# The last stage of a fused attention and MoE kernel: instructions of three engines kept in program order, with another layout of the work in a unit

## The chip, the cores and the metric

One core of one Trainium2 chip runs the whole kernel. The metric is device time in microseconds (us). Before the change the median of three runs is 1489.99 us (1488.47 to 1503.18).

## What is computed

Everything is float32. Attention through 32 packed tokens per head gives 4608 rows of 512 numbers. Two dense blocks follow; the change is in the second.

```python
out = sm_attn(q, sm_attn(p, k, v), sm_attn(p, k, v))   # 8 batches, 8 heads, 576 rows, 64 wide
x = transpose_and_reshape(out)                          # 4608 x 512
r = maximum(x @ w_in, 0);  x = (s * r * r + b) @ w_out  # 512 -> 2048 -> 512
a = x @ w1;  b = x @ w2                                 # 512 -> 1024 each
out = (a * b @ w3) @ w_out2                             # 1024 -> 1024 -> 512
```

## The kernel before

Each float32 operand is split into two parts of fewer bits, hi and lo (`split`, L77 to L81: a cast on ScalarE, ACT, writes hi; a subtraction on VectorE, DVE, writes lo), and each product is three matmuls on TensorE, PE (`mm3`, L83 to L88: lo by hi, hi by lo, hi by hi). Large products use seven smaller ones instead of eight (a Strassen-like scheme), so sums and differences of blocks are formed on DVE beforehand and afterwards.

The kernel has three stages. The first two (attention and the first dense block) take the time up to about 853 us and are left alone. The last stage has three parts.

**w3 times w_out2.** Both weights are multiplied once, so that every row of data meets one matrix in place of two. The loop `for n, m in enumerate(VM)` takes eight blocks of 128 rows of w3. For each, `load_w3` fetches a block two steps ahead, `V_tr` transposes it on PE into PSUM (tile w4t) and splits it into w3T, and `V_mm` runs 24 matmuls of 512 columns into the PSUM tile w4a; from that the seven combinations of the product are formed and split (w4c). At the first step the loop also loads the first piece of the data (`load_x`, tile xb) and eight tiles of weights (`load_w`, tile whl, 256 KB each).

**Units.** The rows are taken in NB3 = 6 pieces j of 768, and each piece in 8 units i of 128 columns of a and b. A unit is seven products (`prod`, 6 x 7 = 42 matmuls of 384 columns, in the order 0, 1, 5, 4, 6, 3, 2) into four PSUM tiles X, Z, Y_ and W. Product 5 adds onto X after ACT has copied X (Ta, L1152), product 6 adds onto it after ACT has copied it again (Ta, L1159), and product 2 adds onto Y_ after DVE has added Y_ to the copy Tb (L1149 behind L1164). At the unit's end DVE multiplies Ta by Tb (L1178) into the tile CA (units 0 to 3) or CB (units 4 to 7). In the last unit of a piece the seven operands of the next piece are split (`split_x`, tile xc).

**y.** The seven products of the previous piece's a * b with w4c are put between the products of a unit as fillers: a chunk (`y_chunk`) is 12 matmuls of 256 columns for one 128-row tile t, three chunks make one of the seven products n, and `y_fin` moves the result out of PSUM (tile yps) into the output sums O. `y_prep` splits the operand of a product into two tiles op of a ring of four; `y_sums` forms the sums of CA and CB (L1187 to L1192). After the last unit of the last piece nothing is left to fill, and the 21 chunks run by themselves: this is the tail. There each chunk is moved out of PSUM by itself.

What sets the order: each engine runs its instructions in the order of the built program, and a scheduler that plans with estimated durations chooses that order. An instruction handed to `tc.keep_in_program_order` stays in the order of the source against the others so marked on its engine. Before the change this holds in the last stage for the first matmul of each product from the second unit on and for the y matmuls, and for nothing on ACT and DVE. All loads and stores here go through one queue of SyncE, SP, in order.

Of the kernel before, what the change touches and what calls it, by code (L numbers as in the profile page):

```python
# [16 lines left out]
ALU = mybir.AluOpType  # L17
# [5 lines left out]
def fused_kernel(  # L23
# [142 lines left out]
    if True:  # L166
# [267 lines left out]
        def pp_split(bp):  # L434
# [3 lines left out]
            for o in range(2):  # L438
                for bb in range(2):
                    c = slice(64 * (bb ^ o), 64 * ((bb ^ o) + 1))  # L440
                    split(hi[:, o::2, c], lo[:, o::2, c], ppT[:, bp, o::2, bb, :], pin=True)
# [502 lines left out]
        def V_tr(m, ps_of):  # L944
            for half in range(2):
                w3T[m, half] = wch_p.tile([P, 2, 4, P], F32R, tag="wph", name="w3T", bufs=4)
                ps = ps_of("w4t")
                for c in range(4):
# [5 lines left out]
                      w3T[m, half][:, 1].rearrange("p a b -> p (a b)"), ps)  # L954
# [103 lines left out]

        def comb_x(j, part):
# [4 lines left out]
            if part == 0:  # L1064
                t1, t2 = (
                    (dec if j == 0 else p3["w4"]).tile(
                        [P, 2, TH], F32, tag="raw" if j == 0 else "xt", name="xt",
                        bufs=RAWB if j == 0 else 2,
                    )
                    for _ in range(2)  # L1070
                )
# [6 lines left out]
        def split_x(j, pr):  # L1078
            src = xt[j][pr]
            if pr == 3:  # L1080
                tt(out=src, in0=src, in1=xt[j][5], op=ALU.subtract)
            t = bp_.tile([P, 2, 2, TH], F32R, tag="xc", name="xc", bufs=7)
            split(t[:, 0], t[:, 1], src)
            xc[j, pr] = t

        def V_mm(m):
            ps = p_ps("w4a")
            for c in range(FB2):
                w = w3T[m, c // 4]
                mm3(ps, w[:, 0, c % 4, :], w[:, 1, c % 4, :],  # L1090
                    *wo2[c], c == 0, c == FB2 - 1)
            i = m % KH
            if m < KH:
# [3 lines left out]
                nc.scalar.copy(p3["b12"], ps[:, NH:])  # L1097
                tt(out=p3["T"][:, 0], in0=p3["b12"], in1=ps[:, :NH], op=ALU.subtract)
                split(w4c[i][:, 0, 0], w4c[i][:, 1, 0], ps[:, :NH])
            else:  # L1100
# [5 lines left out]
                      w4c[i][:, 1, 1:3].rearrange("p a c -> p (a c)"), ps)  # L1106
                split(w4c[i][:, 0, 3:7], w4c[i][:, 1, 3:7], T)
# [21 lines left out]
        O = w4.tile([P, 4, TT, NH], F32, name="O")  # L1129
        C, Y, ops = {}, {}, {}  # L1130

        def prod(j, i, pr, ps, first):
            w = whl.pop((j * FB2 + i, pr))
            for k in range(2):
# [3 lines left out]
                    first and k == 0, k == 1, i + j > 0, skip_group_check=not first)  # L1138
            load_w()

        def unit(j, i, fill, after):
# [10 lines left out]
            nc.scalar.copy(Ta[:, 0], X[:, :TH])  # L1152
            after(0)
# [172 lines left out]
```

## Time and profile before

| | us |
|---|---|
| median of three runs | 1489.99 |
| the profiled execution: its own time | 1485.32 |
| its span | 1483.5 |
| PE busy | 1429.8 |
| DVE busy | 933.9 |
| ACT busy | 756.6 |

The span is one profiled execution, and 1.8 us lie around it. Busy times say which engine works most, not what a wait costs. Matmuls overlap, so how fast PE goes is read from the distance between the starts of matmuls. A wait that PE has is read from the table of waits; the chain of waits shows in order of time what released what.

### The profile page before, as it was taken

The page shows a single profiled execution, that of the slowest core. Times are in us where ns is not written, and L with a number is a line of the kernel's source. Part 1 is how long each engine was busy: PE and PEld are TensorE (multiplying, and loading weights), DVE is VectorE, ACT ScalarE, POOL GpSimd, SP SyncE. Part 2 cuts the span into 40 slices and gives each one's busy share as a digit, 9 for nine tenths or more (in the row PEclk, how much of TensorE's full clock was granted, in tenths as well). Part 3 has the DMA queues.
Part 4 walks back from the last instruction along what each step waited for, and adds up shares of the span by engine and source line. Part 5 has one row for each costly group of instructions (what it writes and reads, how often), then busy time and mean ns, then how long its engine had stood idle before and what let it go on. Part 6 is the DMA issues. An engine that isn't in the chain of part 4 may idle for free.

```text
span 1483.5 us, 28116 instructions
## 1 busy us (share of the span) xinstructions
PE 1429.8 (96%) x10858; PEld 1340.2 (90%) x10858; DVE 933.9 (63%) x1847; ACT 756.6 (51%) x1629; POOL 3.8 (0%) x38
## 2 busy tenths in 40 slices
PE   8999999999999999999999989989999999999996
PEld 5668999999999899998999978989989999899996
DVE  5879544665656766668878364475664856647553
ACT  3677555776566766568766442233422434224322
POOL 0000000000000000000000000000000000000000
PEclk8999999999999999999999999999999999999999
DMA  9967420242353542355635162765756757666541
GB/s 255 253 224 205 128 66 25 63 111 83 98 163 108 162 123 84 111 185 164 201 112 201 59 228 82 241 205 157 227 178 178 233 158 227 177 181 185 160 128 43
DMA packets 179365, 228.87 MB, mean 154 GB/s; under 512 B 55328, under 2 KB 115744, under 8 KB 179232
## 3 DMA queue, kind: packets, MB, share of 16 engines
q1 hardware_dynamic: 179232, 227.07, 51.8%
q8 instruction: 86, 1.41, 0.4%
q14 instruction: 47, 0.39, 0.1%
HBM read 182.98 MB, written 44.04 MB: 153 GB/s over the span
## 4 chain that ended last, share of the span: by engine, by line
PE 88%; DVE 4%; DMA 3%; ACT 2%; issue 1%; SPq 1%; POOL 0%; DVEq 0%; POOLq 0%; ACTq 0%
PE xps L84 9%; PE xps L88 9%; PE xps L87 9%; PE prod L84 7%; PE prod L88 7%; PE prod L87 7%; PE hps L84 4%; PE hps L88 4%; PE hps L87 4%; PE yps L84 4%; PE yps L87 4%; PE yps L88 4%; PE s1p L348 2%; PE scp L202 2%; PE ktp L330 1%; PE ktp L332 1%
## 5 line engine op out<-in xcount | busy, mean ns | idle before, releaser
L88 PE MATMUL xps<-gh,wo 128*128 128x288 f32 (+1 forms) x1024 | 302.5, 299 | 0.0
L87 PE MATMUL xps<-gl,wo 128*128 128x288 f32 (+1 forms) x1024 | 302.3, 298 | 0.0
L84 PE MATMUL xps<-gh,wo 128*128 128x288 f32 (+1 forms) x1024 | 292.0, 300 | 1.6 <-DVE wo L81 1.6
L84 PE MATMUL prod<-xc,whl 128*128 128x384 f32 x672 | 227.7, 339 | 19.3 <-DVE Tb L1149 16.8
L88 PE MATMUL prod<-xc,whl 128*128 128x384 f32 x672 | 225.8, 336 | 0.0
L87 PE MATMUL prod<-xc,whl 128*128 128x384 f32 x672 | 225.6, 336 | 0.0
L87 PEld LDWEIGHTS xps<-gl,wo 128*128 128x128 f32 x1024 | 193.3, 189 | 3.0 <-issue 1.4
L88 PEld LDWEIGHTS xps<-gh,wo 128*128 128x128 f32 x1024 | 193.0, 189 | 2.8 <-issue 1.9
L84 PEld LDWEIGHTS xps<-gh,wo 128*128 128x128 f32 x1024 | 188.5, 189 | 5.0 <-POOL gh L693 2.0
L689 ACT ACTIVATE r<-hps 128x288 f32<-128x288 f32 x256 | 104.4, 410 | 135.2 <-PE hps L88 131.7
L701 DVE TENSOR_TENSOR gl<-r,gh 128x288 fp32r<-128x288 f32 x256 | 115.3, 454 | 78.1 <-ACT r L698 75.5
L84 PE MATMUL hps<-ATh,wpl 128*128 128x288 f32 x512 | 153.9, 301 | 5.9 <-ACT r L689 5.1
L88 PE MATMUL hps<-ATh,wph 128*128 128x288 f32 x512 | 153.0, 299 | 0.0
L87 PE MATMUL hps<-ATl,wph 128*128 128x288 f32 x512 | 152.8, 298 | 0.0
L84 PE MATMUL yps<-w4c,op 128*128 128x256 f32 x504 | 142.3, 282 | 9.8 <-DVE O L1232 2.7
L84 PEld LDWEIGHTS prod<-xc,whl 128*128 128x128 f32 x672 | 126.7, 189 | 25.4 <-DVE Tb L1149 21.7
L1149 DVE TENSOR_TENSOR Tb<-Tb,prod 128x384 f32<-128x384 f32 x96 | 53.0, 553 | 149.6 <-ACT Tb L1164 145.6
L87 PE MATMUL yps<-w4c,op 128*128 128x256 f32 x504 | 142.2, 282 | 0.0
L88 PE MATMUL yps<-w4c,op 128*128 128x256 f32 x504 | 142.2, 282 | 0.0
L87 PEld LDWEIGHTS prod<-xc,whl 128*128 128x128 f32 x672 | 126.8, 189 | 0.0
L88 PEld LDWEIGHTS prod<-xc,whl 128*128 128x128 f32 x672 | 126.7, 189 | 0.0
L698 ACT ACTIVATE r<-r 128x288 f32<-128x288 f32 x256 | 112.6, 444 | 4.8
(166 smaller groups left out, 2582.9 us busy)
## 6 DMA issues: line engine op xcount, KB each, us to landing
whl<-whl SPq DMA_DIRECT2D x336, 256.0 KB, 3.0
raw<-in_moe_w_dram SPq DMA_DIRECT2D x32, 512.0 KB, 4.6
raw<-in_moe_w_out_dram SPq DMA_DIRECT2D x24, 512.0 KB, 4.4
x<-win SPq DMA_DIRECT2D x48, 256.0 KB, 2.8
v<-in_v_dram SPq DMA_DIRECT2D x16, 576.0 KB, 7.0
q<-in_q_dram SPq DMA_DIRECT2D x72, 128.0 KB, 4.4
x<-xst SPq DMA_DIRECT2D x16, 576.0 KB, 3.2
out_dram<-O SPq DMA_DIRECT2D x72, 128.0 KB, 2.4
```

The lines of the kernel that those rows point to most:

```text
L84: ins = nc.tensor.matmul(ps, wl, xh, start=start, stop=False, **kw)
L87: nc.tensor.matmul(ps, wh, xl, start=False, stop=False, **kw)
L88: nc.tensor.matmul(ps, wh, xh, start=False, stop=stop, **kw)
L202: nc.tensor.matmul(ps[sl, c:c + 64], qT[b, t][:, pr, sl], ppT[:, b // 2, pr, b % 2, :], start=True, stop=True,)
L330: nc.tensor.matmul(ps, zero[:, :P], zero, start=True, stop=True)
L332: nc.tensor.transpose(ps[:, jj * TP:(jj + 1) * TP], src[:, 2 * jj:2 * jj + 2, :].rearrange("p j d -> p (j d)"), ident[:TP, :TP],)
L348: nc.tensor.matmul(ps[par][NP * h:NP * (h + 1), :HS], pTd[u // 4][rows, u % 4, NP * h:NP * (h + 1)], kT[u][rows, h], start=True, stop=True,)
L689: nc.scalar.activation(r, ps[:, :HS], AF.Relu)
L698: nc.scalar.activation(r, r, AF.Square)
L701: nc.vector.tensor_tensor(out=gl[:, :HS], in0=r, in1=gh[:, :HS].bitcast(F32), op=ALU.subtract)
L1149: tt(out=out, in0=a, in1=ps[:, :TH], op=ALU.add)
```

## The change

Five things change, all in the last stage.

1. In the last stage every copy, split, sum and add on ACT and DVE, and every first matmul of a product, is kept in the order of the source (helpers `tt` and `cp`, and `pin=True` for `split`).
2. The side work of a unit is given by tables: `FILL` says which chunk of y runs at which of three places of which unit, `SIDE` which operands are split, which sums are formed and where the next piece's differences (`comb_x`) stand. The y work of a piece is spread from the end of unit 0 to unit 6 of the next piece. Before, it stood in units 1 to 6, and at a unit's edges.
3. Of each unit the operands of y are split right behind the copy of product 0, in both halves; the sums stand behind product 5 or product 4.
4. In the tail, products 4 and 5 get PSUM tiles of their own, product 7 starts a fresh one, and the results are moved out once per product or half of it, behind the operands of a later product.
5. The first weight tiles are loaded three at a time in steps 1 to 3 of the w3 loop, and there are nine buffers for them in place of eight.

```diff
-        nc.vector.tensor_tensor(out=lo, in0=src, in1=hi.bitcast(F32), op=ALU.subtract)
+        ins = nc.vector.tensor_tensor(out=lo, in0=src, in1=hi.bitcast(F32), op=ALU.subtract)
+        if pin and pin != "hi":
+            tc.keep_in_program_order(ins)
...
-        WPB = 8
+        WPB = 9
...
-        tt = nc.vector.tensor_tensor
+        def tt(out, in0, in1, op):
+            tc.keep_in_program_order(nc.vector.tensor_tensor(out=out, in0=in0, in1=in1, op=op))
+
+        def cp(out, src):
+            tc.keep_in_program_order(nc.scalar.copy(out, src))
...
         for n, m in enumerate(VM):
...
-                for _ in range(WPB):
+            if n + 1 < FB2:
+                V_tr(VM[n + 1], p_ps, True)
+            if n in (2, 3):
+                comb_x(0, n - 2)
+            if 4 <= n < 4 + 4:
+                for pr in PO[2 * n - 8:2 * n - 6]:
+                    split_x(0, pr)
+            V_mm(m)
+            if 1 <= n < 4:
+                for _ in range(3):
                     load_w()
-            if n + 1 < FB2:
-                V_tr(VM[n + 1], p_ps)
-            V_mm(m)
-            if n in (1, 2):
-                comb_x(0, n - 1)
-            if 3 <= n < 3 + 4:
-                for pr in PO[2 * n - 6:2 * n - 4]:
-                    split_x(0, pr)
...
         def y_tile(n, tail):
-            if n == 4 and tail:
-                a, b = p_ps("yps"), p_ps("yps")
-                return (a, a, b), a
+            if tail and n in (4, 5):
+                return tuple(p_ps("yps") for _ in range(2))
...
+        FILL = {(0, 2): (2, 0)}
+        for e, c in enumerate((n, t) for n in YO[1:] for t in range(TT)):
+            if e:
+                u, f = divmod(e + 2, 3) if e < 15 + 1 else divmod(e + 3, 3)
+                FILL[u, f] = c
+        for t in range(TT):
+            FILL[FB2 - 1, t] = (1, t)
+        SIDE = {
+            (0, 0): (("prep", 2),), (0, 5): (("sum", 1),),
+            (1, 0): (("prep", 4),), (1, 2): (("sum", 3),), (1, 3): (("sum", 2),),
+            (2, 0): (("prep", 6),), (2, 2): (("sum", 4),),
+            (3, 0): (("prep", 7),),
+            (4, 0): (("prep", 5),), (4, 3): (("comb", 0),),
+            (5, 0): (("prep", 3),), (5, 3): (("comb", 1),),
+            (6, 0): (("prep", 1),),
+        }
...
+                        xs = {0: (0,), 1: (1,), 2: (5, "t4"), 3: (4,), 4: (6,), 5: (3,), 6: (2,)}
...
-        for t in range(TT):
-            y_chunk(j, 1, t, True)
-        y_fin(j, 1)
-        for n in YO[1:]:
-            y_prep(j, n)
-            y_sums(j, n)
+        def chunks(n):
             for t in range(TT):
                 y_chunk(j, n, t, True)
-                y_fin(j, n, t)
...
+        chunks(1)
+        y_prep(j, 2)
+        y_sum(j, 1)
+        y_prep(j, 4)
+        fins(1, (), 0)
+        chunks(2)
...
+        chunks(6)
+        fins(6, (2, 3))
+        y_prep(j, 3)
+        fins(6, (), 1)
+        chunks(7)
+        fins(7, (2, 3), hf=1)
+        chunks(3)
+        fins(3, (1,), hf=0)
```

Up to the last stage the built program has the same instructions in the same order on every engine. In the last stage it has the same matmuls. Three places show what moved.

The first place is SP's queue at the start of the w3 loop, from the last load of the first piece's data on (xb is the data, w3st a block of w3, whl the weights of the units). Before:

```order
L1054 DMA xb<-x_1_0_75 128x192
L1041 DMA whl<-whl_89 128x512 x7
L1041 DMA whl<-whl_90 128x512
L942 DMA w3st<-w_5_102 128x1024
L942 DMA w3st<-w_2_99 128x1024
L1054 DMA xb<-x_1_0_75 128x96
L1054 DMA xb<-x_1_1_76 128x288
```

After:

```order
L1062 DMA xb<-x_1_0_75 128x192
L944 DMA w3st<-w_5_102 128x1024
L1049 DMA whl<-whl_89 128x512 x3
L944 DMA w3st<-w_2_99 128x1024
L1049 DMA whl<-whl_89 128x512 x4
L1049 DMA whl<-whl_90 128x512 x2
L944 DMA w3st<-w_6_103 128x1024
L944 DMA w3st<-w_3_100 128x1024
L1062 DMA xb<-x_1_0_75 128x96
L944 DMA w3st<-w_7_104 128x1024
```

The block w_5 now stands ahead of the weight tiles, and these are spread between the blocks of w3.

The second place is DVE at the border of two pieces: from the last product of the unit 7 of a piece (CB is written from Ta and Tb) to the end of unit 0 of the next. Before:

```order
L1178 TENSOR_TENSOR CB<-Ta,Tb 128x2x384
L81 TENSOR_TENSOR xc<-xb,xc 128x768
L1187 TENSOR_TENSOR S_12274<-CA,CB 128x1536
L1149 TENSOR_TENSOR Ta<-Ta,prod 128x384
L81 TENSOR_TENSOR op<-CB,op 128x768 x2
L1072 TENSOR_TENSOR xt<-xb 128x768
L81 TENSOR_TENSOR op<-CB,op 128x768
L1189 TENSOR_TENSOR CA<-CA 128x1536
L1149 TENSOR_TENSOR Tb<-Tb,prod 128x384
L1073 TENSOR_TENSOR xb<-xb 128x2x384
```

After:

```order
L1029 TENSOR_TENSOR CB<-Ta,Tb 128x2x384
L81 TENSOR_TENSOR xc<-xb,xc 128x768
L81 TENSOR_TENSOR op<-CB,op 128x768 x2
L1029 TENSOR_TENSOR Ta<-Ta,prod 128x384
L1029 TENSOR_TENSOR Tb<-Tb,prod 128x384 x2
L1029 TENSOR_TENSOR S_12276<-CA,CB 128x1536
L1029 TENSOR_TENSOR Ta<-Ta,prod 128x384
L1029 TENSOR_TENSOR CA<-Ta,Tb 128x2x384
```

Between CB and the first add into Tb there were a split of xc, the sum S, an add into Ta, three splits of op, one difference xt and the sum CA; there are now a split of xc, two splits of op and one add into Ta. On ACT three casts of op stood in a row between the two copies into Ta there, and two do now.

The third place is DVE in the tail, from the last CB on. Before:

```order
L1178 TENSOR_TENSOR CB<-Ta,Tb 128x2x384
L1187 TENSOR_TENSOR S_12274<-CA,CB 128x1536
L81 TENSOR_TENSOR op<-CB,op 128x768
L1189 TENSOR_TENSOR CA<-CA 128x1536
L81 TENSOR_TENSOR op<-CB,op 128x768
L1232 TENSOR_TENSOR O<-O,yps 128x256
L81 TENSOR_TENSOR op<-CB,op 128x768
L1190 TENSOR_TENSOR CA<-S_12274,CA 128x1536
L1232 TENSOR_TENSOR O<-O,yps 128x256
L81 TENSOR_TENSOR op<-CA,op 128x768
L1232 TENSOR_TENSOR O<-O,yps 128x256
L81 TENSOR_TENSOR op<-CA,op 128x768
```

After:

```order
L1029 TENSOR_TENSOR CB<-Ta,Tb 128x2x384
L81 TENSOR_TENSOR op<-CB,op 128x768 x2
L1029 TENSOR_TENSOR S_12276<-CA,CB 128x1536
L81 TENSOR_TENSOR op<-CB,op 128x768 x2
L1029 TENSOR_TENSOR CA<-CA 128x1536
L81 TENSOR_TENSOR op<-S_12276,op 128x768 x2
L1029 TENSOR_TENSOR CA<-S_12276,CA 128x1536
L1029 TENSOR_TENSOR O<-O,yps 128x768
L81 TENSOR_TENSOR op<-CA,op 128x768 x2
L1029 TENSOR_TENSOR CA<-CB,CA 128x1536
```

The moves out of PSUM (O) stood between the operands of the same product, one per 128-row tile; they now stand behind the operands of a later product, mostly whole.

## Rows read from the trace of the kernel before

**Rows 1.** The page: its head and busy time by engine.

```profile
span 1483.5 us, 28116 instructions
...
PE 1429.8 (96%) x10858; PEld 1340.2 (90%) x10858; DVE 933.9 (63%) x1847; ACT 756.6 (51%) x1629; POOL 3.8 (0%) x38
```

**Rows 2.** Busy time by stretch: stretch, length, engines, granted clock, DMA share, GB/s.

```profile
870.90:875.40 4.50, 4.41 (x15) 3.86 (x16) 4.50 (x7) 1.75 (x3) 0.00 (x0) 0.51 0.70 210
...
987.80:991.20 3.40, 3.35 (x11) 3.35 (x12) 3.40 (x4) 0.00 (x0) 0.00 (x0) 0.52 0.11 36
991.20:1067.00 75.80, 75.80 (x514) 75.80 (x513) 39.38 (x55) 22.71 (x37) 0.00 (x0) 1.00 0.61 174
...
1435.80:1479.10 43.30, 33.44 (x254) 30.58 (x252) 22.64 (x29) 12.43 (x21) 0.00 (x0) 1.00 0.11 28
```

**Rows 3.** Waits of PE in the last stage: total, times, longest.

```profile
PE prod L84 <- DVE Tb L1149: 16.8, 6, 3.5
PE w4t L950 <- DMA w3st<-w: 5.1, 1, 5.1
...
PE prod L84 <- ACT Ta L1159: 1.7, 6, 0.6
```

**Rows 4.** The same table for the first unit alone (915 to 940 us).

```profile
PE prod L84 <- DVE Tb L1149: 1.2, 1, 1.2
PE prod L84 <- ACT Ta L1159: 0.6, 1, 0.6
```

**Rows 5.** Timeline of PE: start, duration, line, operation, tiles.

```profile
976.39 0.34 PE L84 MATMUL prod<-xc,whl 128*128 128x384 f32 x1
...
981.42 0.34 PE L88 MATMUL prod<-xc,whl 128*128 128x384 f32 x1
...
991.60 0.28 PE L84 MATMUL yps<-w4c,op 128*128 128x256 f32 x1
...
993.03 0.34 PE L84 MATMUL prod<-xc,whl 128*128 128x384 f32 x1
```

**Rows 6.** Chain of waits in the w3 loop: start, duration, what.

```profile
860.68 4.15 DMA whl<-whl
864.85 6.00 DMA w3st<-w
870.99 1.94 PE w4t L950 x8
```

**Rows 7.** Timeline of DVE at the first border of two pieces.

```profile
978.22 0.96 DVE L1178 TENSOR_TENSOR CB<-Ta,Tb 128x768 f32<-128x768 f32 x1
...
979.97 1.75 DVE L1187 TENSOR_TENSOR S<-CA,CB 128x1536 f32<-128x1536 f32 x1
...
982.10 1.82 DVE L81 TENSOR_TENSOR op<-CB,op 128x768 fp32r<-128x768 f32 x2
983.84 0.95 DVE L1072 TENSOR_TENSOR xt<-xb 128x768 f32<-128x768 f32 x1
...
985.58 1.75 DVE L1189 TENSOR_TENSOR CA<-CA 128x1536 f32<-128x1536 f32 x1
987.25 0.55 DVE L1149 TENSOR_TENSOR Tb<-Tb,prod 128x384 f32<-128x384 f32 x1
```

**Rows 8.** Timeline of ACT at the same border.

```profile
979.22 2.31 ACT L78 CAST op<-CB 128x768 fp32r<-128x768 f32 x3
981.43 0.47 ACT L1159 COPY Ta<-prod 128x384 f32<-128x384 f32 x1
```

**Rows 9.** Groups by line in the tail: count, busy, mean ns, idle before.

```profile
L84 PE MATMUL yps<-w4c,op 128*128 128x256 f32 x84 | 24.9, 297 | 9.8 <-DVE O L1232 2.7 <-DVE O L1241 2.4 <-DVE O L1239 1.8
...
L81 DVE TENSOR_TENSOR op<-CA,op 128x768 fp32r<-128x768 f32 x6 | 5.7, 955 | 5.1 <-ACT op L78 5.0
```

**Rows 10.** Timeline of SP: six stores of O in a row.

```profile
1428.26 3.87 SPq L1252 DMA_DIRECT2D out_dram<-O  x6
```

**Rows 11.** The page's DMA issues: the stores, to landing.

```profile
out_dram<-O SPq DMA_DIRECT2D x72, 128.0 KB, 2.4
```

More of the change, by code (lines that the diff above doesn't have):

```diff
@@ L1057, in load_x, with xt_pair @@
                 c += n
+        def xt_pair(j):
+            return tuple(
+                (dec if j == 0 else p3["w4"]).tile(
+                    [P, 2, TH], F32, tag="raw" if j == 0 else "xt", name="xt",
+                    bufs=RAWB if j == 0 else 2,
+                )
+                for _ in range(2)
+            )
         def comb_x(j, part):
@@ L1064, in comb_x @@
             if part == 0:
[L1065 to L1071, printed above, removed]
+                t1, t2 = xts.pop(0) if j == 1 else xt_pair(j)
                 tt(out=t1, in0=b12, in1=b11, op=ALU.subtract)
@@ L1129, in fused_kernel @@
         O = w4.tile([P, 4, TT, NH], F32, name="O")
+        xts = [xt_pair(1)]
         C, Y, ops = {}, {}, {}
@@ L1137, in prod, with unit @@
                 mm3(ps[:, :TH], w[:, 0, sl], w[:, 1, sl], x_[:, 0, k], x_[:, 1, k],
-                    first and k == 0, k == 1, i + j > 0, skip_group_check=not first)
+                    first and k == 0, k == 1, True, skip_group_check=not first)
             load_w()
-        def unit(j, i, fill, after):
+        def unit(j, i, fill, side):
             X, Z, Y_, W = (p_ps("prod") for _ in range(4))
@@ L1229, in y_fin, with y_part, add @@
+        def y_part(n, t0, t1):
+            if t0 == 0 and t1 == TT:
+                ps = Y[n][2][:, :TT * NH]
+            else:
+                ps = Y[n][t0 // 2][:, :(t1 - t0) * NH]
+            return ps, [O[:, e, t0:t1].rearrange("p a c -> p (a c)") for e in range(4)]
+        def y_fin(j, n):
+            ps, o = y_part(n, 0, TT)
+            def add(e):
+                tt(out=o[e], in0=o[e], in1=ps, op=ALU.add)
             if n == 1:
-                nc.scalar.copy(o[0], ps)
+                cp(o[0], ps)
@@ L1242, in y_fin @@
-                y_out(j, 1, t0, t1)
-            else:
-                tt(out=o[1], in0=o[1], in1=ps, op=ALU.add)
-                y_out(j, 0, t0, t1)
+                add(3)
+                y_out(j, 1, 0, TT)
+            else:
+                add(1)
+                y_out(j, 0, 0, TT)
         def y_out(j, hf, t0, t1):
@@ L1283, in fused_kernel, with fill @@
-                unit(j, i, fill, after)
-        j = NB3 - 1
-        for t in range(TT):
-            y_chunk(j, 1, t, True)
-        y_fin(j, 1)
-        for n in YO[1:]:
-            y_prep(j, n)
-            y_sums(j, n)
+                if j + 1 < NB3 and i < 4:
+                    load_x(j + 1, (0, 2, 1, 3)[i])
+                def fill(f, j=j, i=i):
+                    jj = j if i == FB2 - 1 else j - 1
+                    if (i, f) in FILL and jj >= 0 and not (i == FB2 - 1 and j == NB3 - 1):
+                        n, t = FILL[i, f]
+                        y_chunk(jj, n, t)
+                        if t == TT - 1:
+                            y_fin(jj, n)
@@ new lines, in side @@
+                def side(f, j=j, i=i):
+                    for what, n in SIDE.get((i, f), ()):
+                        jj = j + (1 if what == "comb" else 0 if n == 1 and what == "prep" else -1)
+                        if 0 <= jj < NB3 and (what != "comb" or jj):
+                            {"prep": y_prep, "sum": y_sum, "comb": comb_x}[what](jj, n)
+                    if i == FB2 - 1 and j + 1 < NB3:
+                        xs = {0: (0,), 1: (1,), 2: (5, "t4"), 3: (4,), 4: (6,), 5: (3,), 6: (2,)}
+                        for pr in xs[f]:
+                            if pr == "t4":
+                                tt(out=xt[j + 1][3], in0=xt[j + 1][3], in1=xt[j + 1][5], op=ALU.subtract)
+                            else:
+                                split_x(j + 1, pr)
@@ L1292, in fused_kernel, with fins @@
+                unit(j, i, fill, side)
+        j = NB3 - 1
+        def chunks(n):
             for t in range(TT):
                 y_chunk(j, n, t, True)
-                y_fin(j, n, t)
+        def fins(n, adds, copy=None, hf=None):
+            for t0, t1 in ((0, TT),) if len(Y[n]) == 3 else ((0, 2), (2, TT)):
+                ps, o = y_part(n, t0, t1)
+                for e in adds:
+                    tt(out=o[e], in0=o[e], in1=ps, op=ALU.add)
+                if copy is not None:
+                    cp(o[copy], ps)
+                if hf is not None:
+                    y_out(j, hf, t0, t1)
@@ new lines, in fused_kernel @@
+        chunks(1)
[4 more added lines that the diff above has]
+        chunks(2)
+        y_sum(j, 3)
+        y_prep(j, 5)
+        y_sum(j, 2)
+        fins(2, (0,))
+        chunks(4)
+        y_prep(j, 6)
+        fins(4, (), 2)
+        y_sum(j, 4)
+        chunks(5)
+        y_prep(j, 7)
+        fins(5, (), 3)
+        chunks(6)
[4 more added lines that the diff above has]
+        fins(7, (2, 3), hf=1)
```

116 lines of the change are left out of this document (45 added, 71 removed).

## The prediction

> **What bounds the kernel now.** First the page: in a span of 1483.5 us PE is busy for 1429.8, DVE for 933.9, ACT for 756.6 [rows 1]. PE is the bound and does the same matmuls after the change, so only time in which PE waits, or runs at a lower clock, can be won; DVE and ACT have room on average and matter where they are late. Next the busy time by stretch: between two borders of pieces, from 991.2 to 1067 us, PE is busy for all of 75.8 us at a granted clock of 1.00 [rows 2]. So a unit in the middle of a piece has nothing to give, and everything must come from a few places. The table of PE's waits in the last stage names them [rows 3]: six waits for an add into Tb (16.8), one for a load of w3 (5.1), six for the second copy Ta (1.7). The rest is the tail, where y's matmuls wait for 9.8 us, most of it for moves into O [rows 9].
>
> A step's price comes from distances of starts, since a matmul's own row overlaps the next. Thirty matmuls of prod start between 976.39 and 981.42: 5.03 / 29 = 0.1735 us each. A chunk of twelve y matmuls takes 993.03 - 991.60 = 1.42, or 0.118 each [rows 5]. A product is then 6 x 0.1735 = 1.04, a unit 42 x 0.1735 = 7.3, and with three chunks 11.5. A wait in the table costs about 0.17 more than it shows: a matmul's row is 0.34 long and the next would have started 0.1735 in.
>
> **The change, part by part.**
>
> *The loads.* The block w_5 stands behind the weight tiles in SP's queue. The chain shows the last of these from 860.68 for 4.15, then w3st for 6.00, and PE's transposes from 870.99 [rows 6]; PE had waited 5.1 [rows 3], so it wanted the block at 865.9. Then the granted clock is 0.51, the 1.2 GHz level, for 4.5 us, after PE had idled [rows 2], which costs 4.5 x 0.49 = 2.2. Together 7.3. Afterwards w_5 is issued where the weight tiles were, at about 860.7; with the 4.15 of the row of the single load it lands at 864.9, one us early; with the 6.00 it lands at 866.7 and is 0.8 late. I take the first, since 6.00 was taken behind eight loads of weights: **gain 7.3**, bounds 4 (a later block is held up in its place, by three weight tiles) and 7.3. The ninth buffer and the order of the differences in this loop are hidden behind V_mm's 24 matmuls per step and cost nothing while these run without a stop; without that cover a difference is 0.95 long [rows 7].
>
> *The borders.* The first unit has one wait of each kind, 1.2 and 0.6 [rows 4]; no y work stands there, and I leave it (0, between -1 and 1). Five borders keep 15.6 and 1.1 us. To these come 10 waits x 0.17 = 1.7 and, at one border, 3.4 us at a clock of 0.52, which cost 1.6 [rows 2]: 20.0. The cause is DVE's order there [rows 7]: between CB, at 978.22, and the add into Tb, at 987.25, stand a split, two sums of 1.75, three op of 0.9, a difference of 0.95: 9.0 us in all, and the longest wait is 3.5. What remains in front of the add afterwards is a split (0.95), two op (1.82) and an add (0.55): 3.3 and a CB of 0.96. That is 5 us less, more than the longest wait, so Tb is no longer late; S follows the adds and is hidden by the three chunks and six products that PE has ahead. If that cover were gone it would cost its 1.75. On ACT three casts of 0.77 and then the copy Ta stood in a row [rows 8]; two casts remain ahead of it, the second of them waiting for CB. So of Ta's wait I keep about 0.5 at each border, 2.4 in all (bounds 0 and 6.5, 1.3 at each). **Gain 17.6**, bounds 13.5 and 20.
>
> *Units 1 to 6.* These waited for nothing. All copies, splits and adds now stand in a fixed order on ACT and DVE, so each new order is a possible wait. DVE has five adds of 0.55, CB's kind of 0.96, two op of 0.95, a sum of 1.75 and a move of about 0.95 at most, some 8.2 us, in a unit of 11.5. On paper, walking each unit through with these durations, no product waits; the nearest is a Tb add in unit 4 with 0.25 us to spare, behind a difference. **Cost 0**, bounds 0 and 15 (the second rival). SP's queue: the loads of weights keep their places between products, and the store of product 5 moves by part of a unit; with a DMA share of 0.61 at most in these stretches [rows 2], I see nothing late.
>
> *The tail.* Before it takes 43.3 us from the first chunk to the last [rows 2] for 252 matmuls, which need 252 x 0.118 = 29.7; to the end of the span it is 47.7. DVE there has 22.6 us of work [rows 2] and some 25 afterwards (joined moves, but operands of the same 0.955 [rows 9] and four sums): less than 29.7, and each operand stands ahead of the moves. So PE runs through. The end is then set by stores: product 7 ends at 6/7 of 29.7 = 25.5, two adds of 0.95 bring 27.4, and SP issues twelve stores at 3.87 / 6 = 0.645 [rows 10], 7.7, up to 35.1; the last lands 2.4 later [rows 11], 37.5, and I add 0.4 for the hand-overs: 37.9. **Gain 9.8**, bounds 6 (two operands each 1.9 late) and 13.5 (the stores catch up).
>
> Here a rule speaks against the change. The rows show moves and stores bunched behind a product that ends late. "Perfetto Trace Analysis" of the Trainium skill, Optimizing Scalar/DVE Operations, says that breaking up instructions may let work complete sooner when ACT or DVE are not saturated but hold up others; the change joins three moves into one. By the rule, with moves by chunk, the stores of product 7 would be out before product 3 ends, and the end would be near 29.7 + 0.4 + 1.3 + 2.4 = 33.8, four us earlier than in my sum. No row before shows the joined form.
>
> **The sum.** 7.3 + 17.6 + 9.8 = 34.7. The profiled execution took 1485.3 of its own, so 1450.6. The ordinary runs shown (1488.5 and 1490.0 with this one) have a mean of 1487.9, 2.6 above it: **1453**.
>
> **The rivals.**
>
> *Forecast, as above, 0.74*: 1447 to 1461, from the bounds of the terms.
>
> *Waits come back in the units, 0.11.* A fixed order lets one late instruction hold up all behind it. If in each of the 35 units with y work a copy or add is late by 0.3 to 0.5, that is 10 to 17: 1463 to 1470. For it: a margin of 0.25 on paper, and the copy at 981.43 that started only when three casts were done [rows 8]. Against it: DVE has 8.2 of work in 11.5.
>
> *A w3 block is still late, 0.04.* The loads of data stand ahead of w_5; if these fill the queue until 866 or later, 5 of the 7.3 stay: 1458.
>
> *The change does not move what waits, 0.05.* If borders keep their 20 because the reason was the room in PSUM and not DVE's order, and tail moves bunch, the loads alone are won and then spent: 1475 to 1490. Against it: the Tb wait ends exactly with the add at 987.25 + 0.55, after DVE had been busy without a gap.
>
> *Slower: ACT blocks product 6 in every unit, 0.06.* In a unit product 5 ends 1.04 + 1.42 + 1.04 + 1.04 = 4.5 us in, and product 6, which needs the copy Ta, is due after a chunk and product 4, at 7.0. The two casts of op now stand ahead of that copy and cannot be passed. If they have to wait for a buffer of op that comes free with the unit's second chunk, at 6.0, they end at 6.0 + 0.2 + 1.5 = 7.7 and the copy at 8.2: 1.2 late, 1.4 with the price of a wait, x 35 units = 49: 1453 + 49 = **1502**. It decides as soon as the casts start later than 7.0 - 0.5 - 1.5 = 5.0 us into a unit. Against it: by the tables the two buffers were last read by the product before the running one, whose last chunk stands in the unit before, so casts can start with the unit. "PSUM — Partial Sum Buffer" of the Trainium skill, Engine vs sequencer instructions, calls ACT's and DVE's queues strict FIFO, which is the mechanism of this rival; the trace agrees as far as the copy behind the three casts goes [rows 8].
>
> **How the numbers follow.** About 1%, 15 us, is what a measurement of this kernel tells from no change: faster means below 1475, slower above 1505; I count the slower rival's 1502 and up, 0.05, as slower, since its 1.4 is rather low (ACT's copies push DVE too). Faster are the first three cases, 0.89. Same are the fourth and a rest of the last: 0.06. The range takes the forecast's own, 1447 to 1461, and most of the second and third: **1446 to 1468**. It leaves out the fourth and fifth case (0.11), the upper end of the second (0.03) and about 0.06 of the first, which its bounds do not hold.
>
> **What would show it.** Right: no wait for w3st near 866 us and no stretch at 0.51 after it; five borders without a wait for Tb, with at most 0.5 for Ta each; PE in the tail at 0.118 us per matmul through 252 of them, and about 8 us from the last matmul to the end of the span. Wrong: rows of prod that wait for ACT or DVE some 35 times, or a tail in which yps waits for op. The prediction fails altogether if the units in the middle of a piece, full before, are not full after.

## The result and the profile after

The changed kernel takes 1452.63 us (median of four runs, 1450.72 to 1456.54). The kernel before, run beside it, has a median of 1494.53 (1488.47 to 1503.18). The ratio is 0.972 (95% interval 0.966 to 0.978): 2.8% faster, and within 0.4 us of the forecast of 1453.

The page of the changed kernel, head and busy times. Against [rows 1] PE does the same 10858 matmuls in a span that is 31.8 us shorter.

```profile
span 1451.7 us, 28061 instructions
...
PE 1422.3 (98%) x10858; PEld 1336.3 (92%) x10858; DVE 939.2 (65%) x1842; ACT 753.1 (52%) x1625; POOL 3.8 (0%) x38
```

PE's waits in the last stage of the changed kernel (total, times, longest). In [rows 3] the same table had 16.8, 5.1 and 1.7 us; the wait for w3st is gone, and the five waits at the borders for Tb too. The longest Ta (1.1) and the only Tb are in the first unit, which stood at 0.6 and 1.2 in [rows 4].

```profile
PE prod L86 <- ACT Ta L1032: 1.8, 5, 1.1
PE prod L86 <- DVE Tb L1029: 0.2, 1, 0.2
```

Busy time by stretch in the changed kernel (columns as in [rows 2]): the place in the w3 loop where PE had waited, the first border, the tail, and what is left behind the tail's last matmul.

```profile
866.00:876.00 10.00, 10.00 (x49) 8.26 (x48) 5.75 (x10) 2.68 (x5) 0.00 (x0) 1.00 0.99 353
975.00:984.00 9.00, 8.89 (x56) 8.57 (x55) 8.60 (x12) 3.22 (x6) 0.00 (x0) 1.00 0.97 296
...
1413.30:1443.00 29.70, 29.70 (x253) 29.70 (x252) 24.25 (x24) 11.70 (x17) 0.00 (x0) 1.00 0.02 6
1443.00:1451.70 8.70, 0.29 (x3) 0.09 (x1) 0.42 (x1) 0.00 (x0) 0.00 (x0) 0.69 0.68 163
```

The granted clock is 1.00 in the first three, where [rows 2] had 0.51 and 0.52 in two places. PE is busy for all of the tail's 29.70 us, against 33.44 of 43.30 before.

DVE at the first border of the changed kernel (start, duration, operation). The first add into Tb now starts 4.1 us after CB, not 9.0 as in [rows 7], and the sum S stands behind it.

```profile
976.17 0.96 DVE L1029 TENSOR_TENSOR CB<-Ta,Tb 128x768 f32<-128x768 f32 x1
...
977.91 1.82 DVE L81 TENSOR_TENSOR op<-CB,op 128x768 fp32r<-128x768 f32 x2
...
980.31 1.21 DVE L1029 TENSOR_TENSOR Tb<-Tb,prod 128x384 f32<-128x384 f32 x2
981.44 1.75 DVE L1029 TENSOR_TENSOR S<-CA,CB 128x1536 f32<-128x1536 f32 x1
```

What is left at the border stands on ACT, as [rows 8] suggested: a cast that waited 0.64 us for CB, and the copy Ta right behind it.

```profile
977.16 0.83 ACT L78 CAST op<-CB 128x768 fp32r<-128x768 f32 x1 [0.64 <-DVE CB L1029]
977.90 0.47 ACT L1032 COPY Ta<-prod 128x384 f32<-128x384 f32 x1
```

The stages are compared by the starts of the same matmuls in each trace. The columns of the table are: "up to w3", the start of the first w4a; "w3 loop", from there to the first prod; "units of piece 0", to the first prod of piece 1; "pieces 1 to 5", to the first yps of the tail; "tail", to the end of the span. All in us.

| | up to w3 | w3 loop | units of piece 0 | pieces 1 to 5 | tail | span |
|---|---|---|---|---|---|---|
| before | 853.8 | 56.35 | 67.25 | 458.4 | 47.7 | 1483.5 |
| changed | 858.2 | 49.10 | 66.7 | 439.3 | 38.3 | 1451.7 |
| e1 loads as before | 859.3 | 57.2 | 66.7 | 439.3 | 38.3 | 1460.9 |
| e2 before, loads changed | 856.8 | 51.2 | 68.8 | 466.6 | 47.7 | 1491.1 |
| e3 sums at the border | 856.9 | 49.4 | 66.8 | 468.9 | 38.3 | 1480.3 |
| e4 one tile for two products | 859.4 | 49.5 | 66.75 | 439.35 | 45.9 | 1460.9 |
| e5 order left free | 855.6 | 51.6 | 66.7 | 449.7 | 38.3 | 1462.0 |
| e6 before, order kept | 853.8 | 58.6 | 66.6 | 450.9 | 64.7 | 1494.6 |
| e7 two op buffers | 859.6 | 49.15 | 66.7 | 470.7 | 48.5 | 1494.6 |
| e8 improved | 859.6 | 49.4 | 63.9 | 437.1 | 36.0 | 1446.0 |
| e9 before once more | 863.3 | 56.4 | 67.2 | 465.4 | 47.7 | 1500.0 |
| e10 as e5, chunk later | 862.4 | 51.5 | 66.8 | 467.5 | 38.3 | 1486.5 |
| e11 changed, chunk later | 857.4 | 49.9 | 66.7 | 441.4 | 38.3 | 1453.7 |
| e12 as e8, SP alone | 858.0 | 49.1 | 63.9 | 437.1 | 38.5 | 1446.5 |

In the last stage the change gives 7.25 + 0.5 + 19.05 + 9.4 = 36.2 us. The first two stages, which it does not touch, took 4.3 longer in this execution, and 36.2 - 4.3 = 31.9 is the difference of the spans.

### The profile page after: what moved, and what is told of

The parts are those of the page before. It is cut to its first block, busy times and chain, and to the rows that moved or that the text cites. A ratio compares the mean times of both kernels' runs of the same rounds, so it can differ in the third digit from the quotient of the medians.

```text
span 1451.7 us, 28061 instructions
## 1 busy us (share of the span) xinstructions
PE 1422.3 (98%) x10858; PEld 1336.3 (92%) x10858; DVE 939.2 (65%) x1842; ACT 753.1 (52%) x1625; POOL 3.8 (0%) x38
## 4 chain that ended last, share of the span: by engine, by line
PE 90%; ACT 3%; DMA 3%; DVE 2%; issue 1%; SPq 0%; POOL 0%; ACTq 0%; POOLq 0%; DVEq 0%
PE xps L86 9%; PE xps L90 9%; PE xps L89 9%; PE prod L86 7%; PE prod L90 7%; PE prod L89 7%; PE hps L86 5%; PE hps L90 4%; PE hps L89 4%; PE yps L89 4%; PE yps L90 4%; PE yps L86 4%; DMA raw<-in_moe_w_in_dram 2%; PE scp L204 2%; PE s1p L350 1%; PE qtp L190 1%
## 5 line engine op out<-in xcount | busy, mean ns | idle before, releaser
L1032 ACT COPY Ta<-prod 128x384 f32<-128x384 f32 x96 | 46.1, 480 | 215.4 <-PE prod L90 214.6
```

The costliest lines, as they stand in the source:

```text
L1032: tc.keep_in_program_order(nc.scalar.copy(out, src))
```

## The experiments

**e1: the loads.** The changed kernel with the loads put back.

```diff
-        WPB = 9
+        WPB = 8
...
                     load_x(0, kk)
+                for _ in range(WPB):
+                    load_w()
...
             V_mm(m)
-            if 1 <= n < 4:
-                for _ in range(3):
-                    load_w()
```

> The changed kernel with only the loads as before: eight weight tiles in the first step of the w3 loop, eight buffers. Theory: the block w_5 again lands behind 2 MB of weights. From the first matmul of w4a to the first of prod 56 us in place of 49.1, with a wait for w3st of about 5 us and a stretch at a granted clock near 0.5; all later parts as in the changed kernel; time 1452.6 + 7 = 1460. Rival: the order kept on ACT and DVE in this loop gave the 7 us, and the loads nothing: 49 to 50 us, no wait for w3st, time 1453.

1459.9 us; the w3 loop takes 57.2, 8.1 more, and nothing else changes. First the wait in e1, then the busy time behind it:

```profile
PE w4t L952 <- DMA w3st<-w: 5.6, 1, 5.6
```

```profile
875.30:882.00 6.70, 5.02 (x16) 4.38 (x17) 3.15 (x5) 1.17 (x2) 0.00 (x0) 0.50 0.66 243
```

A wait of 5.6 and 6.7 us at half clock: the loads' place in SP's queue makes both. The rival, by which the kept order gave these 7 us, falls.

**e2: the loads alone, in the kernel before.**

```diff
-        WPB = 8
+        WPB = 9
...
-                for _ in range(WPB):
-                    load_w()
...
             V_mm(m)
+            if 1 <= n < 4:
+                for _ in range(3):
+                    load_w()
```

> The kernel before with only the loads of the change: three weight tiles in each of steps 1 to 3, nine buffers. Theory: the first matmul of w4a to the first of prod takes 49 us in place of 56.4, everything after it stays (borders some 20 us, tail 47.7): 7 us faster than before, 1482 or so. Rival: another wait takes the place of the one for w_5, because ACT and DVE are still in the scheduler's order: under 2 us.

1489.6 us, 0.4% faster (ratio 0.9958, 0.9933 to 0.9983). The loop gets 5.2 us shorter and not 7.3. Waits of PE in e2, those of the loop and of the borders:

```profile
PE prod L84 <- DVE Tb L1150: 16.8, 6, 3.5
...
PE w4a L84 <- DVE w4c L81: 1.2, 1, 1.2
...
PE w4t L950 <- DMA w3st<-w: 0.4, 1, 0.4
```

With w3st in time, a split of w4c on DVE is late by 1.2, where the order is still free. So the loads are worth 7 only together with the kept order, and about 5 alone. What was not forecast is in the next columns: pieces 1 to 5 take 8 us longer than in the profile of before, with the same table of waits, and e9 takes that up. The units of piece 0 take 1.5 longer, and there too the waits are those of [rows 4], but the clock falls behind them:

```profile
916.60:920.00 3.40, 3.40 (x12) 3.40 (x12) 1.81 (x3) 0.00 (x0) 0.00 (x0) 0.50 0.26 74
```

**e3: DVE's order at the border.** The changed kernel with the sums in front.

```diff
-            (0, 0): (("prep", 2),), (0, 5): (("sum", 1),),
-            (1, 0): (("prep", 4),), (1, 2): (("sum", 3),), (1, 3): (("sum", 2),),
+            (0, 0): (("prep", 2), ("sum", 1), ("sum", 3), ("sum", 2)),
+            (1, 0): (("prep", 4),),
```

> The changed kernel with the three sums of CA and CB (3 x 1.75 us on DVE) moved from units 0 and 1 to the border, ahead of the first adds of unit 0. Theory: what DVE has ahead of the Tb add at the border sets the wait. The first Tb add there starts at 986 in place of 980.3; product 2 is due at about 982.3 and starts 3.9 late: 5 x 4 = 20 us more, 1473 (1470 to 1477 with a stretch at half clock). Rival: a chunk of y now stands ahead of product 2, or ACT's shorter row of casts did it, and DVE's order matters little: 0 to 3 us more, 1453 to 1456.

1482.0 us; pieces 1 to 5 take 29.5 more. DVE at the first border of e3, then PE's waits, then the busy time of one border:

```profile
978.74 1.75 DVE L1029 TENSOR_TENSOR S<-CA,CB 128x1536 f32<-128x1536 f32 x1
980.52 1.76 DVE L1029 TENSOR_TENSOR CA<-CA 128x1536 f32<-128x1536 f32 x1
982.31 1.76 DVE L1029 TENSOR_TENSOR CA<-S,CA 128x1536 f32<-128x1536 f32 x1
...
984.45 1.21 DVE L1029 TENSOR_TENSOR Tb<-Tb,prod 128x384 f32<-128x384 f32 x2
```

```profile
PE prod L86 <- DVE Tb L1029: 18.7, 6, 3.7
```

```profile
1172.60:1179.00 6.40, 5.86 (x21) 5.86 (x22) 2.92 (x6) 1.62 (x3) 0.00 (x0) 0.50 0.31 80
```

The waits are those of the theory: 18.7 - 0.2 over five borders, 3.7 each against 3.9 forecast. The rest, some 10 us, is the clock: behind each of the five waits it falls to half for 3.3 to 6.8 us, some 23 in all. I had counted a few us for that; it is a third of the price.

**e4: the tail's banks.** The changed kernel with product 4 in the tile of product 2.

```diff
-            if tail and n in (4, 5):
+            if tail and n == 5:
```

> The changed kernel with product 4 of the tail in the PSUM tile of product 2, in place of two tiles of its own. Theory: PE must wait in the tail until product 2 has been moved into O, which stands behind the operands of product 5 on DVE: that move ends 13.3 us into the tail, product 4 is due at 8.5, so one wait of yps for O of 4.8 us and a tail of 43 in place of 38.3 us, 1457. Rival: the order of the moves, not the banks, made the tail short: the move is early enough or the wait is made up at the stores, under 1.5 us more.

1462.6 us; the tail takes 45.9, 7.6 more. The wait in e4 and the busy time behind it:

```profile
PE yps L86 <- DVE O L1029: 4.7, 1, 4.7
```

```profile
1427.50:1434.30 6.80, 5.91 (x28) 5.94 (x29) 0.75 (x1) 0.00 (x0) 0.00 (x0) 0.50 0.00 0
```

4.7 were counted as 4.8; the other 3 us are again a stretch at a granted clock of 0.50. One tile shared gives back 7.6 of the tail's 9.4, so here a move that stands behind operands needs a PSUM tile of its own. What the joined moves are worth by themselves no run separates.

**e5: the kept order taken away.** The changed kernel with ACT and DVE left to the scheduler.

```diff
         def tt(out, in0, in1, op):
-            tc.keep_in_program_order(nc.vector.tensor_tensor(out=out, in0=in0, in1=in1, op=op))
+            nc.vector.tensor_tensor(out=out, in0=in0, in1=in1, op=op)
 
         def cp(out, src):
-            tc.keep_in_program_order(nc.scalar.copy(out, src))
+            nc.scalar.copy(out, src)
...
-                split(t[:, 0], t[:, 1], src[:, h * KH // 2:(h + 1) * KH // 2], pin=True)
+                split(t[:, 0], t[:, 1], src[:, h * KH // 2:(h + 1) * KH // 2])
```

(and the other five splits of the stage in the same way)

> The changed kernel with its layout, loads and tiles, but copies, splits, sums and adds of the last stage on ACT and DVE left to the scheduler; PE keeps its order. At the border DVE then has the sum S, an op, a difference and another sum between CB and the first Tb add again. Theory: the kept order is what frees the border, the layout alone does not: 3 to 4 us at each of five borders come back, perhaps a few in the w3 loop: 1470 to 1478. Rival: the layout (a chunk ahead of product 2, operands split early) carries most: under 5 us more, below 1458.

1465.0 us, between the theory and its rival. The w3 loop takes 2.5 more, pieces 1 to 5 take 10.4 more, the tail nothing. The wait for Tb in e5:

```profile
PE prod L86 <- DVE Tb L1029: 8.8, 6, 2.1
```

The scheduler puts S, an op, a difference and a sum ahead of the Tb add as before, but the longest wait is 2.1 and not 3.5. That is 1.4 less, the length of one chunk, and at no border of e5 (waits of 1.2 to 2.1 us) does the clock fall. e10 and e11 test the chunk.

**e6: the kept order alone, in the kernel before.** The helpers `tt` and `cp` of the change, its argument `pin=True` for all splits of the last stage, and True for the first matmuls, in the kernel before; layout, loads and tail are untouched.

```diff
-        tt = nc.vector.tensor_tensor
+        def tt(out, in0, in1, op):
+            tc.keep_in_program_order(nc.vector.tensor_tensor(out=out, in0=in0, in1=in1, op=op))
+
+        def cp(out, src):
+            tc.keep_in_program_order(nc.scalar.copy(out, src))
...
-            nc.scalar.copy(Ta[:, 0], X[:, :TH])
+            cp(Ta[:, 0], X[:, :TH])
```

> The kernel before with its layout, loads and tail, but with the last stage's ACT and DVE instructions and first matmuls kept in the order of the source. At the border DVE then has a split, two op and an add between CB and the Tb add. Theory: the borders lose most of their 20 us (2 to 5 remain); the loads' 7.3 stay; the tail gets longer, since moves and operands of a product now wait for one another in turn, 47.7 to 50 to 58 us: in sum 1470 to 1480. Rival: without the new layout the kept order makes waits in the units (operands of y in one row with the copies): above 1488.

1503.1 us, 0.6% slower than before (ratio 1.0063, 1.0037 to 1.0089), so the forecast of 1470 to 1480 was wrong. The profiled execution, which the table of stages shows, was the shortest of ten (1496.4). Waits in e6, and ACT at its first border:

```profile
PE yps L86 <- DVE op L81: 12.0, 6, 2.7
PE prod L86 <- ACT Ta L1031: 9.3, 6, 1.6
...
PE yps L86 <- DVE O L1028: 4.9, 8, 0.9
```

```profile
982.67 1.63 ACT L78 CAST op<-CB 128x768 fp32r<-128x768 f32 x2
984.21 0.48 ACT L1031 COPY Ta<-prod 128x384 f32<-128x384 f32 x1
```

No Tb wait is left at the borders, as the theory said; but about 1.6 us per border of Ta took its place, since the copy stands behind two casts that are later here. The tail takes 17 us more than before, and not the 2 to 10 I had allowed. Operands and moves in the order of the source wait for one another: PE's waits there are 18.3 (the 12.0 and 4.9 above and 1.4 for ACT's copies) in place of the 9.8 of [rows 9]. The other half is the clock, which [rows 2] has at 1.00 in the tail of before; in e6 it is at half for 13.6 and then for 6.8 us, of which the first is:

```profile
1437.80:1451.40 13.60, 10.73 (x45) 9.55 (x44) 7.45 (x8) 0.63 (x2) 0.00 (x0) 0.50 0.00 0
```

So the rival's number holds, but not its place: the waits stand at the borders and in the tail, not in the units between. Kept order is worth what the written order is worth.

**e7: the slower rival.** The changed kernel with half the buffers of op.

```diff
-                t = w4.tile([P, 2, KH // 2, TH], F32R, tag="op", name="op", bufs=4)
+                t = w4.tile([P, 2, KH // 2, TH], F32R, tag="op", name="op", bufs=2)
...
-            (6, 0): (("prep", 1),),
+            (6, 5): (("prep", 1),),
```

> The changed kernel with two buffers of op in place of four (and the operands of product 1 split behind product 3 of unit 6 in place of at its start). It makes what the slower rival of the prediction needs: in units 1 to 5 of pieces 1 to 5 the casts wait for the second chunk of the unit, with the copy Ta behind them on ACT. That rival's price is 1.4 us in each of 25 units, 35, and in the tail each of six products waits about 1.9 for its operands, 11: 1453 + 46 = 1499, slower than before. If ACT's row of casts does not hold up product 6 (the copy gets past, or there is more room than counted), only the tail's part shows: 1464.

1493.8 us, as slow as before (ratio 1.0004, 0.999 to 1.0019). Waits in e7, and ACT in one unit:

```profile
PE prod L86 <- ACT Ta L1032: 9.3, 31, 1.1
PE yps L86 <- DVE op L81: 7.3, 6, 1.3
PE yps L86 <- DVE O L1029: 7.3, 5, 1.5
PE prod L86 <- DVE Tb L1029: 4.6, 10, 0.6
```

```profile
1004.58 1.57 ACT L78 CAST op<-CA 128x768 fp32r<-128x768 f32 x2 [3.78 <-PE yps L90]
1006.05 0.47 ACT L1032 COPY Ta<-prod 128x384 f32<-128x384 f32 x1
```

The mechanism of the rival is real: the casts wait for PE's chunk, the copy stands behind them, and PE waits for it 31 times, 25 of them in units 1 to 5. Its price was too high, though: such a wait is about 0.3 us in the table and some 0.55 between starts of matmuls, not 1.4, which makes 14 us and not 35. Pieces 1 to 5 lose 31.3 us all the same, because five moves into O (8.5 us between starts) and nine adds into Tb (6.8) come late as well. The tail takes 10.2 more, of the 11 counted. With four buffers none of this is to be seen in the changed kernel. The Trainium skill ("PSUM — Partial Sum Buffer", Engine vs sequencer instructions) calls these queues strict FIFO; the rows of ACT agree, the copy starting as the second cast ends.

**e8: a version that beats both.** The changed kernel with four edits.

```diff
             prod(j, i, 4, Y_, True)
+            if j == 0:
+                cp(Tb[:, 1], Y_[:, :TH])
...
-            add(Tb[:, 1], Tb[:, 0], Y_)
+            if j == 0:
+                tt(out=Tb[:, 1], in0=Tb[:, 0], in1=Tb[:, 1], op=ALU.add)
+            else:
+                add(Tb[:, 1], Tb[:, 0], Y_)
...
+                    eng = nc.scalar if o and tail else nc.sync
...
-                    nc.sync.dma_start(
+                    eng.dma_start(
...
-            (0, 0): (("prep", 2),), (0, 5): (("sum", 1),),
+            (0, 0): (("prep", 2, (0,)),), (0, 2): (("prep", 2, (1,)),), (0, 5): (("sum", 1),),
...
-            for t0, t1 in ((0, TT),) if len(Y[n]) == 3 else ((0, 2), (2, TT)):
+            for t0, t1 in ((0, TT),) if len(Y[n]) == 3 and n != 7 else ((0, 2), (2, TT)):
```

> The changed kernel with four edits meant to beat it: in the tail product 7 is moved out in two parts (two row tiles, then one) and the last twelve stores are issued half by SP, half by ACT; at the border the second operand of product 2 is split behind product 5 in place of product 0, so that the copy Ta is no longer behind a cast that waits for CB; in piece 0 ACT copies Y_ before product 6 is added. By the times of the changed kernel: the end of the span 33.9 us after the first matmul of the tail in place of 38.3 (-4.4), the borders' waits for Ta of 0.33 gone (-1.6), the waits for Tb of 0.28 in the units of piece 0 gone (-2): 8 us less, 1444.6. If SP's issue is not what sets the end, the tail gains under 1 us; if stores on two queues share the same landing, about 2.

1445.9 us (1443.8 to 1449.6), a ratio of 0.9687 (0.9661 to 0.9713) to before. The stages show that it gains on the changed kernel: piece 0 2.8, pieces 1 to 5 2.2, the tail 2.4. Piece 0 and the borders gave a little more than expected (2 and 1.6); the tail gave 2.4 and not 4.4. DVE's adds of product 7, SP's six stores with the longest and the last four of them, ACT's longest store, and the DMA issues from 1437 us on (KB each, us to landing) in e8:

```profile
1435.80 1.95 DVE L1029 TENSOR_TENSOR O<-O,yps 128x512 f32<-128x512 f32 x4 [0.71 <-PE yps L90]
```

```profile
1437.12 5.12 SPq L1277 DMA_DIRECT2D out_dram<-O  x6
```

```profile
1437.75 1.75 SPq L1277 DMA_DIRECT2D out_dram<-O  x1
```

```profile
1439.61 2.62 SPq L1277 DMA_DIRECT2D out_dram<-O  x4
```

```profile
1437.89 1.63 ACTq L1277 DMA_DIRECT2D out_dram<-O  x1
```

```profile
out_dram<-O SPq DMA_DIRECT2D x6, 128.0 KB, 3.0
out_dram<-O ACTq DMA_DIRECT2D x6, 128.0 KB, 3.2
```

Two of the durations that I used did not hold. With two queues at work a store lands 3.0 us after its issue on SP and 3.2 on ACT (medians of six), not 2.4 [rows 11]. And six stores take 5.12 on SP in place of the 3.87 of [rows 10], since one of them takes 1.75 (on ACT one takes 1.63). The 5.12 / 6 = 0.85 is therefore not what a store costs beside a second queue: the last four on SP take 2.62 / 4 = 0.655 each, about as with SP alone. Splitting product 7 gained next to nothing: its first add starts 1435.80 - 1410.04 = 25.8 us into the tail, when the whole product is done (25.5), although its first two row tiles were done 1.4 earlier. In the kernel they share one PSUM tile with the third, which is the likely reason; no run gave them a tile of their own.

**e9: the kernel before once more.** No edit but two blank lines, which move the line numbers.

> The kernel before once more, unchanged. Its runs lie between 1486 and 1503 us, those of the changed kernel between 1451 and 1457. Theory: the waits at the borders are the same each time (Tb 16.8 us in six, Ta 1.7), but whether TensorE's granted clock falls to half behind them is not: the profile of before shows one such stretch at the borders, the kernel with only the loads changed five. So this profile has the same table of waits, pieces 1 to 5 take longer than 458.4 us by half of the length of the additional stretches, and a run of 1490 to 1500 has two to five of them. Rival: the spread comes from the transfers of the first two stages: pieces 1 to 5 take 458 again and the part up to the first matmul of w4a differs from 853.8 us by what the time does.

The profiled execution took 1501.8 us, 16.4 more than the first. The waits of e9:

```profile
PE prod L86 <- DVE Tb L1151: 16.9, 6, 3.5
...
PE prod L86 <- ACT Ta L1161: 1.7, 6, 0.6
```

They are those of [rows 3]. Busy time in three of the five stretches behind the borders of e9:

```profile
997.20:1000.90 3.70, 3.62 (x12) 3.62 (x13) 3.70 (x5) 0.00 (x0) 0.00 (x0) 0.55 0.16 45
...
1277.00:1283.80 6.80, 5.35 (x19) 5.36 (x20) 6.69 (x8) 0.48 (x1) 0.00 (x0) 0.50 0.38 119
1372.70:1376.00 3.30, 3.30 (x11) 3.30 (x12) 3.06 (x4) 0.00 (x0) 0.00 (x0) 0.50 0.10 11
```

All five borders end at half clock here, some 20 us in all (the first window, with a mean of 0.55, reaches a little past its stretch); the first profile had one such stretch of 3.4. Half of the additional 17 is 8.5, and pieces 1 to 5 took 7.0 longer. The other 9.5 us lie in the first two stages. So theory and rival each have a part: with the same waits pieces 1 to 5 take 458 us in one execution and 465 in another.

**e10 and e11: the chunk in unit 0.** The first is made in e5, the second in the changed kernel. The edit moves the first chunk from unit 0 to unit 1, and the fifteen chunks behind it one place later:

```diff
-        FILL = {(0, 2): (2, 0)}
+        FILL = {}
         for e, c in enumerate((n, t) for n in YO[1:] for t in range(TT)):
-            if e:
-                u, f = divmod(e + 2, 3) if e < 15 + 1 else divmod(e + 3, 3)
-                FILL[u, f] = c
+            u, f = divmod(e + 3, 3)
+            FILL[u, f] = c
```

> The kernel without the kept order on ACT and DVE (pieces 1 to 5: 449.7 us), and the first chunk of y not in unit 0 but in unit 1 as before. Theory: that chunk, 1.42 us of PE work ahead of product 2 of unit 0, is the half of the border's gain which the layout gives: without it the Tb wait is 3.5 in place of 2.1 at each border, and stretches at half clock come back: 457 to 467 us. Rival: another part of the layout gives it (operands split early, sums later): 449 to 451.

> The changed kernel (pieces 1 to 5: 439.3 us) with the first chunk of y in unit 1 as before, its kept order untouched. Theory: with DVE's order kept the first Tb add ends about when product 2 is then due, so the chunk is not needed: 0.3 us at each border, 439 to 441 in all. Rival: chunk and order are both needed: 1.4 more at each border, 446 or more.

1479.4 and 1454.8 us. PE's waits for Tb, in e10 and then in e11:

```profile
PE prod L86 <- DVE Tb L1029: 15.8, 6, 3.5
```

```profile
PE prod L86 <- DVE Tb L1029: 0.2, 1, 0.2
```

Both theories hold, each by half a microsecond over the top of its range. With the order free the chunk is worth 17.8 us in the profiled executions: the longest wait goes from 2.1 back to 3.5 (7 in all), and half clock comes back at all five borders. The profiled execution of e10 was the longest of six (1488.3); by the medians it is 14.4. With the order kept the chunk is worth 0.4 per border, 2.1 in all.

**e12: e8 with SP alone.**

```diff
-                    eng = nc.scalar if o and tail else nc.sync
+                    eng = nc.sync
```

> The improved kernel (tail 35.97 us to the end of the span) with all of its last twelve stores on SP again, product 7 still moved out in two parts. If the second queue gave the gain: twelve stores of 0.645 from 24 us in, with a landing of 2.4, end at 37 and the tail takes 37 to 38. If each store takes longer because two queues share the way out (0.85 each in the improved kernel), SP alone does as well: 36.

The tail takes 38.5, as in the changed kernel; SP's stores in e12:

```profile
1435.15 8.60 SPq L1277 DMA_DIRECT2D out_dram<-O  x12
```

```profile
1435.79 1.31 SPq L1277 DMA_DIRECT2D out_dram<-O  x1
```

They start 27.1 us into the tail (1435.15 - 1408.08), not 24, and need 8.60 in one queue. The second queue gave all of the tail's 2.4, so the rival falls. One store takes 1.31 here as well, with no second queue beside it; why single stores in e8 and e12 take so long stays open. By the medians (1448.5 and 1445.9) the two kernels can hardly be told apart; the stages can.

## Why the prediction was right

*The loads*: forecast 7.3, measured 7.25 and, by e1, 8.1. One thing was missing: alone they are worth 5.2 (e2), since with w3st in time a split is late that the kept order puts right. And one row was misread: 4.15 is the row of a weight tile of 256 KB, while w_5 has 512. In the changed kernel w_5 is issued at 865.05 and lands 4.9 later:

```profile
w3st<-w SPq DMA_DIRECT2D x1, 512.0 KB, 4.9
```

That is 869.95, and PE's transposes of it start at 870.09: it came in time by 0.1 us, not by one. In e11, with the same loads, PE waits 0.7 for it. So the term came out at its full size by a narrow margin.

*The borders*: forecast 17.6, measured 19.05 between the two profiles. The reason was the right one: with the sums put back ahead of the Tb add, pieces 1 to 5 lose 29.5 (e3), and with DVE's order kept the chunk in unit 0 adds only 2.1 (e11). The prediction does not name that chunk, which is worth 14 to 18 where the order is left free (e10 against e5). The term was small by 1.5. Measured against e8, whose borders have no wait left, pieces 1 to 5 lost 458.4 - 437.1 = 21.3 before, where the sum has 20.0, and lose 2.2 in the changed kernel, where it keeps 2.4.

*The units in the middle*: cost 0, and no wait of them is in the table, nor one for a load. (The DMA share of 0.61, which the prediction reads as the most in these stretches, is the mean of one of them.) That is not quite the same as no loss: in piece 0 the adds into Tb held up PE by some 0.4 us in each unit between starts of matmuls, before and after the change alike, and e8 gained 2.8 there. The first unit, left at 0, gained 0.5. The case in which waits come back did not happen; e7 shows what that hung on, since with two buffers of op in place of four the same order costs 31 us.

*The tail*: forecast 37.9 us in all, measured 38.3; PE 29.7 of 29.7, and 8.6 behind the last matmul where 8 were said. SP's twelve stores, in the changed kernel:

```profile
1440.95 7.92 SPq L1271 DMA_DIRECT2D out_dram<-O  x12
```

They begin 1440.95 - 1413.31 = 27.6 into the tail (27.4 forecast) and take 7.92 (7.7).

*The rule on breaking up instructions* (the Trainium skill, "Perfetto Trace Analysis", Optimizing Scalar/DVE Operations) would have put the tail at 33.8. In the form tried in e8 and e12 the smaller moves started the stores at 27.1 in place of 27.6 and left the end where it was (38.5 in e12), since the first of them still started only when the whole product was done; what gave something was a second queue. With a tile of its own for each part it was not tried, so the rule is not refuted.

*The sum against the runs*: the forecast time came true, the base did not. I put the ordinary runs of before 2.6 us over the profiled one, by a mean that leaves out the third run, 1503.2; the median over all its runs is 1494 to 1496, about 10 over. e9 shows two parts of that: 7 us in pieces 1 to 5, where the clock falls behind the border waits, and 9.5 in the first two stages. The changed kernel has no such waits left, so the first part does not come back in it: its runs lie within 6 us (1450.7 to 1456.5), those of before within 17 (1485.9 to 1503.1). The changed kernel had four runs, though, and the other some sixty, so the narrower range shows little by itself. The gain against ordinary runs is 42 us, where the terms say 36 against one execution that was a favourable one. That 1453 was met within 0.4 us is therefore luck: a base 7 too low and a gain 7 too low cancel. With the median as base the same sum would have given 1494.5 - 34.7 = 1460, 7 us too long.

## What to carry to other kernels

Price a wait of PE by its row and by the clock behind it: here waits of 2.6 to 3.7 us cost up to about twice their length, and not in every execution, so one profile of a kernel with such waits can look better than its median. Write the order of the in-order engines by hand only together with the layout: the same rule of order made this kernel faster with a new layout and slower with the old one (e6). At a border the order takes away nearly all of the wait for Tb, and one chunk of PE work ahead of the late step takes away about half of it (15.8 to 8.8 us) and the half clock behind it. When PE has no gaps left, look at what comes behind its last matmul: here the stores on one queue.

## What the hardware showed unexpectedly

The waits at the five borders of the kernel before are the same in both of its profiles, 2.6 to 3.5 us, but the granted clock fell to 0.5 (the 1.2 GHz level) behind one of them in one execution and behind all five in the other, for 3.3 to 6.8 us. Behind the waits of 1.2 to 2.1 us in e5 it fell at none; but in e2 it fell behind the first unit's waits of 0.6 and 1.2 us, behind which it did not fall in the two profiles of before. When SP and ACT stored at the same time, stores of 128 KB landed 3.0 and 3.2 us after their issue, against 2.4 with SP alone; issuing twelve took 5.4 us on the two queues (e8), and 8.60 (e12) and 7.92 (changed kernel) on one.
